# A new order of issue for the pieces of attention and feed-forward, from the third product with w_in on

## The chip, the cores and the metric

One core of one Trainium2 chip runs the kernel. The metric is the device time of one execution in microseconds (us), lower is better. The five engines of the core (TensorE as PE, with its weight loads as PEld; VectorE as DVE; ScalarE as ACT; GpSimd as POOL; SyncE as SP, which here only issues DMAs) each work through an instruction stream of their own, in order, and wait for one another through semaphores.

## The reference

```python
q_s = softmax over d of q;  k_s = softmax over s of k      # 8 batches, 8 heads, 576 rows, 64 wide
kv  = einsum('bhsd,bhse->bhde', k_s, v)
x   = einsum('bhsd,bhde->bhse', q_s, kv)                   # 4608 tokens x 512
h   = x @ w_in                                             # 512 x 2048
g   = maximum(h, 0) + log1p(exp(-abs(h)))                  # softplus
out = g @ w_out                                            # 2048 x 512
```

All arrays are float32.

## The kernel before

**Arithmetic.** The two large products are computed to float32 accuracy on the matrix engine by writing each operand as a high part and a low part (`hi` a rounded copy, `lo` the remainder); one product then is three matmuls, hi·hi, lo·hi and hi·lo, added up in one bank of PSUM. A cast on ACT makes the high part and a subtraction on DVE the low part.

**Tiling.** The 4608 tokens are nine tiles of 512 (t = 0 to 8). The 2048 columns of w_in are sixteen blocks of 128 (j = 0 to 15).

- Tiles 0 to 2 go one by one. `U` (L715) is the product of one tile with one column block, 12 matmuls; `A` (L732) is softplus on ACT; `G` or `H` (L736) splits the result (ACT L740, DVE L743); `O` or `I` (L748) is its product with one block of w_out, 12 matmuls into four banks, `I` a half of it. In the token `U21`, 21 is 16·t + j.
- Tiles 3 to 8 go in three pairs p = 0 to 2, each pair by a scheme of seven products in place of eight (Strassen's). `C p.s.i` (L825) are the pieces of the product with w_in for the s-th of eight double blocks: i = 0 to 6 the products (six matmuls each, L852 to L854, 1.36 us), 7 `spread` (ACT, copies bank 0 to bank 1 between product 0 and products 1 or 2), 8 `take` (ACT, L868, reads bank 1 between products 1 and 3), 9 and 14 softplus out of a bank, 10 `half` (ACT, reads bank 1 between products 3 and 5), 11 and 15 additions on DVE (L875, L879), 12 and 16 softplus in place. `d p.i.s` (L959) are the products with w_out, six matmuls, L966 to L968; `e p.i.s.0` and `.1` (L935) split their right operand (ACT L946, DVE L949); `t` (L929) are differences that the scheme needs; `o` (L970) ends a pair: copies, sums and transposes (L1003) on DVE and ACT, and `store`, each four DMA issues on POOL (L1009).
- `X p.c.name` (L792) prepares the right operands of a pair's `C` products: differences on DVE (L816), casts on ACT (L809), subtractions on DVE (L813).

**Attention.** `k b.h.i` (L462) are the nine steps of one pair of heads (maximum, reduced over the partitions on POOL for later batches, exponent on ACT, product 6 of 20 matmuls at L528), `q` the softmax of the queries, `x t.h.i` (L656) the product of queries and kv (step 3, eight matmuls at L651), its ACT copy (step 6, L675) and, for the first tiles, the split (4, 5).

**Weights.** `T`, `M`, `S`, `J`, `P`, `Q` unpack one column block of both weights from the form in which it was loaded; they run on ACT (about 1.1 us each), DVE (1.2 us) and, with `.1`, POOL (2.5 us). This takes place in the first 150 us.

**Transfers.** `R2.n` (`fetch_sums`, L379) fetches 1 MB of sums of weight blocks for n = 8·p + s into one of two buffers, `x2` and `x0` in turn; so it can start only when the last product with the sums of s − 2 (`C` pieces 1, 3, 4 and 5) has read that buffer, and `C p.s.1` is the first product that needs it. `R0`, `R3`, `R4` fetch other weight parts, `r p.n` (L908) a block of weights for `d` by four DMAs, `n` (`kv_prefetch`, L1056) keys and values ahead of their `k` steps, `L` (`q_load`, L551) the queries of a tile by four DMAs of 256 KB. All of these are issued by SP, in the order of their tokens; the stores of `o` are issued by POOL.

**What sets the order.** The string `ORDER` holds 2304 tokens. The loop at the end of `tile_attn_ffn` hands each to `do` (L1091), which emits its instructions, under `tc.manual_schedule()`: the order of the tokens is the order of issue on every engine. Waits follow from the buffers that the pieces read and write.

Of the kernel before, what the change touches and what calls it, by code (L numbers as in the profile page):

```python
# [9 lines left out]
U8 = mybir.dt.uint8  # L10
U16 = mybir.dt.uint16
U32 = mybir.dt.uint32
# [55 lines left out]
    O16 Y0.1 G18 Y1.0 q2.6 q2.8 k2.0.7 k2.1.7 k2.1.8 U21 A21 Y1.2 k2.2.0 Y0.3 U22 O17 G19 q2.3 D6 Y1.1 k2.0.8 Y1.3 O18
    G20 Y3.0 k2.3.0 O19 A22 G21 O20 G22 k2.3.1 Y3.1 k2.2.1 Y3.2 Y0.4 k2.2.2 q2.5 Y2.0 Y2.1 O21 D8 O22 k2.2.3 k2.3.2
    k2.3.3 k2.3.4 k2.3.5 k2.2.4 q2.7 L3 D15 Y4.0 U23 k2.2.5 Y2.2 Y2.3 k2.3.6 k2.2.6 q2.9 A23 H1.7.0 H1.7.1 k2.2.7  # L70
    k2.3.7 U24 A24 Y2.4 Y2.5 q2.10 U25 Y4.2 O23 U26 H1.8.0 k2.2.8 x2.0.0 Y1.4 H1.8.1 A25 q3.0 q3.1 q3.12 H1.9.0 q2.11
    Y3.3 n k3.0.0 Y2.6 O24 D13 Y2.7 U27 Y3.4 k2.3.8 H1.9.1 x2.2.0 x2.1.0 Y1.5 Y4.1 Y3.5 Y4.3 O25 A26 H1.10.0 Y4.4 n
    Y0.5 k3.1.0 Y3.6 A27 U28 A28 Y1.6 H1.11.0 H1.10.1 x2.1.3 x2.0.4 x2.0.5 O26 Y2.8 Y3.7 H1.12.0 U29 q3.2 Y6.0 q3.3
    H1.11.1 x2.1.4 x2.1.5 x2.3.0 D11 O27 Y0.6 Y0.7 H1.12.1 A29 U30 k3.0.4 k3.0.5 k3.1.4 q3.5 k3.1.5 Y4.5 Y1.7 O28 q3.4
    q3.6 R0.0 H1.13.0 A30 H1.14.0 U31 Y3.8 Y4.6 x2.3.3 A31 q3.7 Y0.8 H1.13.1 L4 O29 H1.14.1 q3.8 x2.2.4 Y6.1 q3.13
    R0.1 x2.2.5 R0.2 x2.3.4 x2.3.5 k3.0.6 y0.0 y0.1 q3.9 H1.15.0 y0.2 y0.3 H1.15.1 k3.1.6 k3.0.7 k3.0.8 U32 A32 n n
    q4.0 q4.1 q4.12 y0.4 R0.3 Y6.2 k3.1.7 O30 H2.0.0 H2.0.1 Y6.3 Y1.8 q4.2 U33 k3.1.8 O31 F1.0 k3.2.0 k3.3.0 R2.0
    k3.2.4 k3.3.4 R0.4 U34 A33 H2.1.0 U35 F1.1 q3.10 k3.3.5 q4.3 k3.2.5 k3.2.6 F1.2 q4.4 F1.3 q4.6 k3.3.6 Y7.0 n Y7.1
    A34 y0.5 y1.0 Y5.0 Y6.4 O32 k3.2.7 k3.2.8 Y6.5 y0.6 k3.3.7 k3.3.8 A35 H2.1.1 y2.0 R0.5 x3.0.0 x3.1.0 O33 R0.6 Y4.7
    Y4.8 U36 Y7.2 H2.2.0 H2.3.0 H2.2.1 O34 y1.1 y1.2 y1.3 y1.4 y0.7 U37 H2.3.1 q3.11 n A36 A37 H2.4.0 x3.2.0 H2.4.1  # L80
    y0.8 x3.1.3 x3.0.6 x3.1.6 x3.3.0 Y5.2 O35 H2.5.0 k4.0.0 k4.1.0 k4.0.4 R0.7 q4.5 U38 O36 x3.3.3 x3.3.6 x3.2.6 U39
    R0.8 q4.7 Y7.3 k4.0.5 y3.0 y3.1 H2.5.1 k4.1.4 k4.1.5 k4.0.6 k4.1.6 y2.1 R0.9 Y7.4 Y7.5 k4.0.7 O37 A38 y3.2 y3.3
    k4.1.7 k4.1.8 y1.5 y3.4 y3.5 H2.6.0 y4.0 y4.1 y4.2 U40 y4.3 H2.6.1 k4.0.8 O38 A39 H2.7.0 U41 n q4.8 y4.4 y1.6
    k4.2.0 Y6.6 Y6.7 n H2.7.1 O39 k4.3.0 y3.6 k4.2.4 y2.2 R0.10 q4.13 Y7.6 R0.11 A40 A41 k4.3.4 Y7.7 k4.3.5 U42 H2.8.0
    Y7.8 R0.12 q4.9 q4.10 k4.2.5 H2.8.1 k4.2.6 k4.2.7 y4.5 H2.9.0 A42 k4.3.6 k4.3.7 O40 k4.2.8 Y6.8 Y5.1 Y5.3 y1.7
    y1.8 y2.3 Y5.4 Y5.5 H2.10.0 y4.6 x4.0.0 U43 H2.9.1 Y5.6 Y5.7 A43 X0.0.hB11 O41 X0.0.lB11 U44 k4.3.8 H2.11.0 R0.13
    H2.10.1 H2.11.1 y4.7 O42 x4.1.0 x4.1.3 x4.0.6 X0.0.T1 y5.0 x4.1.6 A44 q4.11 Y5.8 U45 y5.1 y5.2 x4.2.0 O43 X0.0.hT1
# [5 lines left out]
    C0.0.9 R3.2.0 X0.1.lT1 X0.0.lT4 C0.0.3 C0.0.10 C0.1.0 F2.1 y5.7 X0.1.lT3 C0.1.7 X0.1.T4 X0.1.hT4 X0.0.lT3 C0.0.4
    y5.8 k5.0.0 X0.1.lT4 L5 C0.0.5 R2.2 y7.2 y7.3 C0.1.1 C0.0.11 C0.0.6 k5.1.0 C0.1.8 C0.1.2 k5.0.4 C0.1.3 C0.0.15
    R4.2.0 C0.2.0 F2.2 C0.1.4 R3.3.0 k5.1.4 k5.1.5 C0.1.10 y6.3 y6.4 k5.0.5 k5.0.6 q5.0 q5.1 k5.1.6 C0.1.5 n R2.3
    C0.0.14 C0.2.7 C0.2.1 C0.2.8 C0.1.11 C0.1.6 R4.5.0 k5.0.7 k5.0.8 y6.5 R4.3.0 C0.2.2 R3.4.0 C0.2.3 k5.1.7 k5.1.8
    q5.12 n C0.1.15 R4.4.0 C0.1.9 e0.0.0.0 C0.3.0 q5.2 q5.3 C0.2.10 C0.1.14 C0.2.4 k5.2.0 k5.2.4 C0.3.7 q5.4 C0.2.5
    C0.2.11 q5.5 C0.3.1 R2.4 t0.1.1 C0.2.6 C0.2.15 C0.3.2 R3.5.0 e0.0.1.0 y6.6 y6.7 y6.8 k5.3.0 C0.3.8 C0.3.3 q5.6
    C0.2.9 C0.4.0 C0.3.4 C0.3.10 C0.3.5 C0.2.14 C0.4.7 e0.0.0.1 C0.4.1 k5.3.4 q5.7 C0.3.11 k5.2.5 q5.8 k5.3.5 k5.2.6
    k5.3.6 C0.3.14 C0.3.6 C0.4.8 C0.4.2 C0.4.3 y7.4 y7.5 y7.6 q5.13 C0.3.9 k5.2.7 k5.3.7 k5.3.8 C0.5.0 y7.7 C0.4.4  # L100
    q5.9 q5.10 C0.3.15 L6 q6.0 C0.4.10 C0.5.7 q6.1 k5.2.8 C0.4.11 C0.4.5 x5.0.0 R2.5 C0.5.1 C0.5.8 C0.4.9 C0.4.14
    C0.1.16 C0.4.6 C0.5.2 q5.11 n C0.3.16 C0.5.9 t0.1.2 C0.5.3 k6.0.0 k6.0.4 C0.5.10 R3.6.0 C0.1.12 x5.1.0 C0.6.0
# [5 lines left out]
    e0.0.3.1 C0.7.4 C0.7.11 e0.0.4.0 e0.0.4.1 C0.7.5 d0.0.1 C0.7.6 C0.0.12 q6.6 d0.0.2 X1.0.hB21 e0.0.5.0 k6.2.0
    k6.3.0 t0.1.0 e0.0.5.1 d0.0.3 r0.1 d0.0.4 d0.0.5 q6.5 k6.3.4 e0.0.6.0 e0.0.6.1 d0.0.6 k6.2.4 q6.7 e0.0.7.0 k6.3.5
    e0.0.7.1 X1.0.lB11 k6.2.5 e0.3.0.0 e0.3.1.0 e0.3.0.1 e0.3.1.1 C0.7.14 t0.2.1 k6.2.6 k6.2.7 k6.3.6 e0.3.2.0  # L110
    e0.3.2.1 d0.0.7 C0.6.12 e0.3.3.0 t0.2.0 r0.2 d0.3.0 e0.3.4.0 d0.3.1 e0.3.5.0 C0.7.15 t0.1.7 k6.3.7 C0.7.16 t0.2.2
    o0.spread.0 e0.3.4.1 C0.2.16 e0.3.3.1 d0.3.2 e0.3.6.0 t0.2.3 d0.3.3 o0.spread.1 d0.3.4 r0.5 e0.3.7.0 q6.8 e0.3.5.1
    d0.3.5 e0.1.0.0 e0.1.1.0 e0.3.6.1 t0.2.6 d0.3.6 C0.7.12 e0.3.7.1 d0.3.7 e0.1.0.1 e0.1.1.1 r0.4 d0.1.0 q6.13 t0.2.4
    k6.3.8 r0.6 e0.1.2.0 q6.9 t0.3.1 d0.1.1 r0.7 e0.1.3.0 t0.2.5 e0.1.2.1 q6.10 d0.1.2 e0.1.3.1 d0.1.3 k6.2.8 t0.2.7
    r0.11 n e0.1.4.0 e0.1.4.1 e0.1.5.0 e0.1.5.1 e0.1.6.0 o0.v.0 e0.1.7.0 d0.1.4 e0.2.0.0 x6.0.0 d0.1.5 e0.1.6.1 d0.1.6
    e0.1.7.1 d0.1.7 e0.2.2.0 t0.3.5 e0.2.1.0 e0.2.0.1 X1.1.hB21 o0.u.1 d0.2.0 t0.3.3 e0.2.1.1 d0.2.1 t0.3.2 o0.u.0
# [1100 lines left out]
```

## Time and profile before

| | |
|---|---|
| median of 3 runs | 824.14 us (823.71 to 824.73) |
| the profiled execution | 824.4 us, of which the span of the trace is 822.6 us |
| granted TensorE clock, mean | 0.997 |
| PE busy | 801.7 us, 97% of the span |
| DVE, ACT, POOL busy | 71%, 60%, 14% |
| DMA | 193.74 MB, 236 GB/s over the span |

Times in the rows are microseconds from the start of the span. A row of an engine's timeline is: start, duration, engine, line, operation, output<-input, tile, count, and in brackets the idle time of the engine before it with what ended that. Matmuls overlap: one of 128x512 is shown with some 0.39 us, but the next one starts 0.23 us after it, so time lost on PE is read from start to start.

### The profile page before, as it was taken

The page shows a single profiled execution, that of the slowest core. Times are in us where ns is not written, and L with a number is a line of the kernel's source. Part 1 is how long each engine was busy: PE and PEld are TensorE (multiplying, and loading weights), DVE is VectorE, ACT ScalarE, POOL GpSimd, SP SyncE. Part 2 cuts the span into 40 slices and gives each one's busy share as a digit, 9 for nine tenths or more (in the row PEclk, how much of TensorE's full clock was granted, in tenths as well). Part 3 has the DMA queues.
Part 4 walks back from the last instruction along what each step waited for, and adds up shares of the span by engine and source line. Part 5 has one row for each costly group of instructions (what it writes and reads, how often), then busy time and mean ns, then how long its engine had stood idle before and what let it go on. Part 6 is the DMA issues. An engine that isn't in the chain of part 4 may idle for free.

```text
span 822.6 us, 12090 instructions
## 1 busy us (share of the span) xinstructions
PE 801.7 (97%) x4312; PEld 637.2 (77%) x4312; DVE 584.1 (71%) x934; ACT 497.3 (60%) x824; POOL 116.0 (14%) x211
## 2 busy tenths in 40 slices
...
GB/s 305 374 291 233 262 114 246 212 211 205 270 297 365 230 375 285 310 311 311 178 248 268 129 235 170 299 254 128 244 172 200 165 192 165 281 118 291 264 124 90
DMA packets 118236, 193.74 MB, mean 236 GB/s; under 512 B 8416, under 2 KB 90592, under 8 KB 108960
## 3 DMA queue, kind: packets, MB, share of 16 engines
...
## 4 chain that ended last, share of the span: by engine, by line
PE 82%; DMA 6%; DVE 5%; ACT 3%; POOL 2%; issue 2%; SPq 1%; POOLq 0%; ACTq 0%; DVEq 0%
PE po L852 6%; PE po L968 6%; PE po L853 5%; PE po L854 5%; PE po L966 5%; PE po L967 5%; PE ph L725 4%; PE ph L726 4%; PE po L767 4%; PE ph L727 4%; PE po L769 4%; PE po L768 4%; PE ph L852 3%; PE ph L854 3%; PE ph L853 3%; PE ph L966 3%
## 5 line engine op out<-in xcount | busy, mean ns | idle before, releaser
L1011 POOL DMA_DIRECT2D out<-w x92 | 59.4, 653 | 296.4 <-DVE w L1003 291.9
L767 PE MATMUL po<-w,g_hi 128*128 128x512 f32 x164 | 65.2, 398 | 2.1 <-ACT g_hi L740 2.1
L725 PE MATMUL ph<-x,w 128*128 128x512 f32 x164 | 65.5, 400 | 0.0
L769 PE MATMUL po<-w,g_lo 128*128 128x512 f32 x164 | 64.4, 393 | 0.4 <-DVE g_lo L743 0.3
L949 DVE TENSOR_TENSOR g_lo<-w,g_hi 128x512 fp32r<-128x512 f32 x74 | 49.5, 685 | 20.6 <-ACT g_hi L946 20.6
L768 PE MATMUL po<-w,g_hi 128*128 128x512 f32 x164 | 64.0, 390 | 0.0
L726 PE MATMUL ph<-x,w 128*128 128x512 f32 x164 | 64.0, 390 | 0.0
L727 PE MATMUL ph<-x,w 128*128 128x512 f32 x164 | 63.9, 390 | 0.0
L946 ACT CAST g_hi<-w 128x512 fp32r<-128x512 f32 x74 | 45.5, 619 | 19.1 <-PE po L967 12.8
L933 DVE TENSOR_TENSOR w<-w,w 128x512 f32<-128x512 f32 x72 | 48.5, 683 | 2.7 <-ACT w L886 1.7
L946 ACT CAST w<-w 128x512 fp32r<-128x512 f32 x52 | 31.8, 619 | 24.8 <-PE po L967 18.1
L875 DVE TENSOR_TENSOR w<-po,w 128x512 f32<-128x512 f32 x24 | 16.5, 687 | 40.8 <-PE po L854 40.8
L743 DVE TENSOR_TENSOR g_lo<-g,g_hi 128x512 fp32r<-128x512 f32 x46 | 31.1, 683 | 19.3 <-ACT g_hi L740 19.1
...
L852 PE MATMUL po<-w,x 128*128 128x512 f32 x112 | 44.3, 396 | 0.0
L854 PE MATMUL po<-w,x 128*128 128x512 f32 x112 | 43.8, 391 | 0.0
L853 PE MATMUL po<-w,x 128*128 128x512 f32 x112 | 43.7, 390 | 0.0
L734 ACT ACTIVATE g<-ph 128x512 f32<-128x512 f32 x48 | 28.4, 598 | 24.9 <-PE ph L727 24.6
L477 DVE TENSOR_REDUCE mx<-kvt 128x128 f32<-128x640 f32 x28 | 36.8, 1319 | 4.9 <-DMA kvt<-in_kv_tail 4.0
L949 DVE TENSOR_TENSOR w<-w,w 128x512 fp32r<-128x512 f32 x52 | 35.2, 686 | 6.4 <-ACT w L946 6.2
L767 PEld LDWEIGHTS po<-w,g_hi 128*128 128x128 f32 x164 | 30.8, 188 | 11.4 <-ACT g_hi L740 3.9
L740 ACT CAST g_hi<-g 128x512 fp32r<-128x512 f32 x46 | 28.2, 620 | 18.3 <-PE po L768 13.5
...
## 6 DMA issues: line engine op xcount, KB each, us to landing
x<-sums SPq DMA_DIRECT2D x24, 1024.0 KB, 5.7
...
kept<-w SPq DMA_DIRECT2D x15, 1024.0 KB, 6.9
w<-kept SPq DMA_DIRECT2D x13, 1024.0 KB, 8.7
x<-sums_out SPq DMA_DIRECT2D x44, 256.0 KB, 5.1
w<-kept SPq DMA_DIRECT2D x36, 256.0 KB, 4.6
x<-kept SPq DMA_DIRECT2D x36, 256.0 KB, 4.6
w<-sums_out SPq DMA_DIRECT2D x36, 256.0 KB, 5.7
```

What stands on the lines that cost most here:

```text
L725: nc.tensor.matmul(ph, lhsT=w_hi, rhs=x_hi, start=h == 0, stop=False)
L726: nc.tensor.matmul(ph, lhsT=w_lo, rhs=x_hi, start=False, stop=False)
L727: nc.tensor.matmul(ph, lhsT=w_hi, rhs=x_lo, start=False, stop=h == HP - 1)
L767: nc.tensor.matmul(po, lhsT=g_hi[:, ms], rhs=w_hi, start=j == 0, stop=False)
L768: nc.tensor.matmul(po, lhsT=g_hi[:, ms], rhs=w_lo, start=False, stop=False)
L769: nc.tensor.matmul(po, lhsT=g_lo[:, ms], rhs=w_hi, start=False, stop=j == NJ - 1)
L852: nc.tensor.matmul(ph, lhsT=w_hi, rhs=x_hi, start=c == 0 and i in (0, 4), stop=False, **more)
L853: nc.tensor.matmul(ph, lhsT=w_lo, rhs=x_hi, start=False, stop=False, **more)
L854: nc.tensor.matmul(ph, lhsT=w_hi, rhs=x_lo, start=False, stop=c == 1, **more)
L946: nc.scalar.copy(ring[p, i, s][0], right_of(p, i, s))
L949: engine.tensor_tensor(out=lo, in0=right_of(p, i, s), in1=hi.bitcast(F32), op=ALU.subtract)
L966: nc.tensor.matmul(bank, lhsT=w_hi, rhs=hi, start=begin, stop=False, **more)
```

## The change

Only the string `ORDER` changes. It holds the same 2304 tokens as before, so each engine gets the same instructions; the first 129 tokens (up to `U2`, the third product with w_in) stand as they were, and nearly all behind them stand in another order. The new one comes from a search over a model of the engines in which a wait is for a whole buffer. The matmuls of one piece stay together; what changes is which piece follows which, on every engine and on the SP queue. Of the 2304 tokens the places that matter below, before and after:

```diff
@@ -56,143 +56,142 @@
-    P3 Q3 A1 M5 k1.0.8 U2 S5.1 A2 k1.1.3 k1.1.4 U3 P4 O1 A3 G2 G3 M7.1 O2 T8 J5 Q4 q1.0 P5 Q5.1 q1.1 O3 k1.1.5 M6.1
-    q1.2 T6 J6 U4 q1.4 M8.1 k1.1.6 k1.1.7 T7 J7 U5 P6 A4 Q6 U6 k1.2.0 M10 G4 J8 O4 k1.2.1 P7 Q7 A5 G5 U7 T9 k1.1.8 A6
-    k1.3.0 P8 Q8 k1.3.1 T10 k1.2.2 T12 O5 q1.3 G6 O6 k1.2.3 A7 S10 k1.3.2 M9 k1.3.3 S9 M12.1 J9 q1.6 U8 J10 G7 O7
...
-    O12 x1.1.3 x1.0.4 x1.0.5 G13 G14 Q15.1 P0 x1.2.0 O13 U15 x1.1.4 x1.1.5 x1.3.0 L2 D4 Q0.1 k2.1.0 x1.3.3 x1.2.4
...
-    y2.7 y2.8 X0.1.hB22 O45 X0.1.hB21 y3.7 y3.8 X0.1.lB21 A46 X0.1.lB22 A47 C0.0.0 X0.1.T3 R2.1 n X0.1.hT3 H2.14.0
-    X0.1.T2 H2.14.1 I2.14.0 X0.0.lB21 I2.14.1 H2.15.0 X0.0.T2 X0.0.hT2 X0.0.lT2 X0.1.hT2 X0.1.lT2 C0.0.7 C0.0.1
...
-    x5.3.0 e0.0.1.1 C0.4.12 R2.7 t0.1.4 R4.7.0 C0.7.7 C0.7.1 C0.0.16 C0.5.15 x5.3.3 x5.2.6 x5.3.6 k6.0.6 C0.6.11
-    C0.6.14 R4.6.0 C0.6.6 e0.0.2.0 C0.7.8 C0.6.9 r0.0 n C0.7.2 k6.0.7 e0.0.2.1 C0.6.15 e0.0.3.0 k6.0.8 k6.1.6 C0.7.3
...
-    X1.0.hB22 X1.0.T3 X1.0.lB22 X1.0.T2 X1.0.hT2 X1.0.lT1 X1.0.lT2 X1.0.hT3 x6.3.6 d0.6.0 d0.6.1 e0.6.4.0 o0.flip.0.1
-    o0.store.0.1 e0.6.3.0 e0.6.3.1 C1.0.0 C1.0.7 o0.c12.0 o0.flip.3.0 e0.6.4.1 e0.6.5.0 X1.0.lB21 e0.6.5.1 d0.6.2
-    X1.1.T3 R3.1.1 e0.6.6.0 X1.1.hB22 X1.0.lT3 d0.6.3 e0.6.7.0 r0.13 d0.6.4 X1.1.lB22 X1.1.T2 X1.1.hT2 e0.6.6.1
-    X1.1.hT1 X1.1.T4 e0.6.7.1 d0.6.5 d0.6.6 X1.1.lT2 d0.6.7 k7.0.0 o0.c21.0 C1.0.1 C1.0.2 X1.0.T4 X1.0.hT4 C1.0.8
...
-    C1.0.6 C1.1.2 k7.0.5 C1.1.3 k7.1.5 k7.0.6 q7.1 q7.12 q7.2 q7.3 k7.1.6 C1.0.14 C1.2.0 C1.1.4 L8 o0.flip.2.1 C1.1.10
-    C1.1.5 q7.4 q8.0 R4.1.1 C1.2.7 R2.10 n C1.2.1 C1.0.12 C1.2.8 C1.1.11 C1.1.6 o0.flip.2.0 C1.2.2 q8.1 R3.3.1 n
-    C1.2.3 C1.1.14 C1.0.15 C1.1.9 C1.3.0 k7.2.0 k7.2.4 q7.5 q7.7 k7.3.0 C1.2.4 C1.2.10 o0.store.2.0 C1.3.7 q7.6 C1.2.5
-    R2.11 o0.flip.3.1 C1.3.1 R4.3.1 C1.2.11 R3.4.1 C1.2.6 C1.3.2 R4.5.1 C1.2.9 C1.1.15 q7.8 C1.3.8 R2.12 q7.13 q7.9
...
-    o1.u.0 d1.4.0 e1.4.3.0 t1.3.5 t1.4.5 d1.4.1 e1.4.4.0 e1.4.5.0 e1.4.2.1 d1.4.2 o1.c11.0 X2.0.lB21 e1.4.3.1 e1.4.4.1
-    e1.4.5.1 d1.4.3 d1.4.4 d1.4.5 x8.3.3 x8.2.6 X2.0.hB22 X2.0.lB22 e1.4.6.0 e1.4.6.1 e1.5.0.0 r1.10 e1.4.7.0 x8.3.6
-    e1.5.0.1 e1.4.7.1 X2.1.T1 d1.4.6 X2.1.hB22 X2.1.T3 e1.5.2.0 X2.1.lB22 e1.5.2.1 e1.5.1.0 e1.5.1.1 d1.4.7 o1.c22.1
...
+    P3 Q3 A1 M5 k1.0.8 U2 T8 k1.1.3 k1.1.4 U3 P4 A2 q1.0 S5.1 T9 Q4 A3 G2 M6.1 O1 J5 G3 U4 k1.1.5 P5 O2 T6 M8.1 Q5.1
+    k1.1.6 M7.1 T7 k1.2.0 k1.2.1 J6 J8 P6 k1.1.7 k1.2.2 q1.1 U5 A4 Q6 A5 J7 O3 U6 G4 G5 P7 M10 Q7 k1.1.8 O4 M9 q1.2
+    T12 k1.3.0 U7 S9 q1.3 P8 A6 Q8 J9 T11 T10 A7 G6 q1.4 k1.3.1 O5 D4 P9 k1.2.3 G7 S10 M14.1 k1.2.4 q1.6 k1.3.2 O6
...
+    x1.0.0 A12 G11 U13 Q14 M15.1 k1.2.8 J15 x1.2.0 k1.3.7 P15 k1.3.8 Q15.1 U14 x1.1.0 A13 G12 D3 x1.1.3 O11 x1.3.0 U15
+    G13 x1.0.4 x1.1.4 O12 x1.1.5 A14 x1.0.5 P0 Q0.1 k2.0.0 D6 G14 x1.3.3 D5 x1.2.4 k2.1.0 O13 x1.2.5 x1.3.4 P1 L2
...
+    H2.14.1 X0.0.T2 C0.0.0 I2.14.1 C0.0.7 X0.1.hT3 X0.1.lB21 y7.1 X0.1.hT1 H2.15.0 R4.2.0 X0.1.lB22 X0.1.T2 k5.1.5
+    y5.7 C0.0.2 X0.0.hT3 R4.0.0 I2.14.0 H2.15.1 I2.15.1 X0.1.T4 y7.0 R4.3.0 X0.1.hT2 I2.15.0 k5.1.6 y6.2 X0.1.lT2
...
+    C0.6.9 n C0.0.16 C0.5.12 C0.7.1 C0.7.2 k6.0.0 x5.3.3 C0.6.14 e0.0.2.0 n C0.7.4 e0.0.2.1 k6.0.4 r0.0 q6.6 e0.0.3.0
+    C0.7.8 x5.2.6 k6.1.0 d0.0.0 k6.0.5 C0.6.11 d0.0.1 q6.8 q6.5 R4.6.0 x5.3.6 k6.1.4 e0.0.4.0 q6.7 k6.1.5 C0.7.3
+    C0.7.10 k6.0.6 k6.1.6 d0.0.2 t0.1.4 k6.0.7 e0.0.3.1 r0.1 C0.7.9 e0.0.5.0 d0.0.3 R4.7.0 e0.0.4.1 k6.1.7 e0.0.5.1 n
...
+    X1.1.T1 e0.5.4.0 x6.2.6 X1.0.T1 e0.5.1.1 t0.4.2 d0.5.1 e0.5.2.1 e0.5.4.1 X1.0.T3 x6.3.6 e0.5.3.1 d0.5.2 X1.0.hB22
...
+    d0.5.7 X1.0.hT1 X1.0.hT4 X1.0.lT1 e0.6.4.0 e0.6.3.0 d0.6.1 e0.6.3.1 e0.6.5.0 d0.6.2 d0.6.3 C1.0.2 e0.6.5.1
+    o0.c12.1 X1.1.lT2 e0.6.7.0 X1.1.T4 R3.1.1 X1.1.hT3 e0.6.4.1 X1.1.lT1 d0.6.4 e0.6.6.0 e0.6.6.1 X1.0.lT2 e0.6.7.1
+    R2.9 C1.0.1 C1.0.9 R3.2.1 d0.6.5 o0.flip.1.0 n o0.flip.1.1 d0.6.6 d0.6.7 C1.0.8 o0.c21.0 k7.0.0 X1.1.lT3 o0.c12.0
...
+    X1.0.lT4 X1.1.hT4 X1.1.lT4 C1.1.0 o0.flip.2.0 k7.1.0 C1.1.7 o0.flip.3.1 k7.0.4 L7 o0.c21.1 C1.0.4 k7.1.4 R4.0.1
+    C1.0.3 C1.1.2 C1.0.10 C1.1.1 C1.0.5 R3.3.1 C1.2.0 C1.1.4 C1.0.14 o0.flip.3.0 C1.0.11 R2.10 o0.store.1.0 C1.1.8
+    q7.0 C1.1.3 e1.0.0.0 q7.1 C1.2.7 q7.12 C1.0.6 q7.2 q7.4 C1.0.15 R4.2.1 C1.2.2 C1.1.9 C1.1.10 C1.1.11 C1.1.5 C1.3.0
+    R4.1.1 q7.3 C1.2.9 R4.4.1 R2.11 C1.1.14 e1.0.1.0 C1.2.1 C1.1.6 k7.0.5 C1.3.7 C1.2.4 C1.3.2 L8 C1.3.1 k7.1.5 C1.2.8
...
+    e1.2.7.1 d1.2.6 e1.4.0.1 o1.v.1 o1.u.1 X2.0.lB11 d1.2.7 x8.3.3 e1.4.2.0 e1.4.2.1 d1.4.0 e1.4.1.1 e1.4.3.0 e1.4.4.0
+    e1.4.3.1 d1.4.1 t1.4.6 X2.1.T1 e1.4.4.1 d1.4.2 x8.3.6 e1.4.5.0 t1.4.4 e1.4.6.0 d1.4.3 e1.4.7.0 e1.4.5.1 r1.9
...
+    R2.18 R3.3.2 C2.1.5 C2.3.0 o1.store.0.0 R4.1.2 C2.2.1 C2.2.8 R2.19 C2.1.14 C2.3.7 C2.1.11 C2.1.6 C2.0.15 C2.2.2
+    o1.flip.2.1 C2.4.7 R2.20 C2.5.0 C2.4.1 C2.2.15 C2.4.8 C2.4.2 C2.4.4 R4.3.2 C2.4.3 C2.3.11 t2.1.3 R2.21 C2.0.12
+    C2.5.2 R2.22 C2.6.0 C2.4.14 C2.6.7 C2.5.9 C2.4.6 C2.4.15 C2.5.5 R3.7.2 C2.6.1 C2.6.2 C2.5.4 C2.6.4 R4.6.2 C2.4.12
...
```

## Rows read from the trace of the kernel before

**Rows 1.** Page of the profile, busy time of each engine over the span.

```profile
PE 801.7 (97%) x4312; PEld 637.2 (77%) x4312; DVE 584.1 (71%) x934; ACT 497.3 (60%) x824; POOL 116.0 (14%) x211
```

**Rows 2.** Windows: length, busy of PE, PEld, DVE, ACT, POOL; clock, DMA share, GB/s.

```profile
40.00:80.00 40.00, 40.00 (x182) 29.83 (x181) 35.71 (x44) 38.94 (x48) 5.54 (x6) 1.00 0.87 281
...
480.30:500.30 20.00, 18.42 (x89) 13.82 (x89) 19.09 (x30) 11.03 (x21) 6.98 (x10) 1.00 0.57 166
...
680.00:720.00 40.00, 40.00 (x176) 32.74 (x176) 9.68 (x15) 15.01 (x28) 15.40 (x24) 1.00 0.71 223
```

**Rows 3.** Timeline of PE around the longest wait.

```profile
515.25 0.39 PE L854 MATMUL po<-w,x 128*128 128x512 f32 x1
518.32 0.76 PE L852 MATMUL ph<-x,x 128*128 128x512 f32 x1 [2.68 <-DMA x<-sums]
...
521.34 0.40 PE L853 MATMUL po<-w,spare 128*128 128x512 f32 x1
```

**Rows 4.** Timeline of PE at seven other waits.

```profile
117.64 0.50 PE L767 MATMUL po<-w,g_hi 128*128 128x512 f32 x1 [1.19 <-ACT g_hi L740]
...
247.66 0.50 PE L769 MATMUL po<-w,g_lo 128*128 128x512 f32 x1 [0.31 <-DVE g_lo L743]
...
321.21 0.50 PE L767 MATMUL po<-w,g_hi 128*128 128x512 f32 x1 [0.90 <-ACT g_hi L740]
...
401.35 0.80 PE L528 MATMUL att<-kvt 128*64 128x65 f32 x20 [0.76 <-ACT w L675]
...
493.85 0.50 PE L968 MATMUL po<-w,spare 128*128 128x512 f32 x1 [1.33 <-DVE w L949]
...
637.67 0.50 PE L966 MATMUL po<-w,spare 128*128 128x512 f32 x1 [1.84 <-ACT w L946]
...
650.23 0.50 PE L968 MATMUL po<-w,w 128*128 128x512 f32 x1 [0.25 <-DVE w L949]
```

**Rows 5.** Timeline of the SP queue ahead of the longest wait.

```profile
504.24 2.65 SPq L561 DMA_DIRECT2D qt<-in_q  x4
...
507.64 0.55 SPq L382 DMA_DIRECT2D x<-sums  x1
```

**Rows 6.** DMA issues near 318, 508, 712, 721 us: KB each, us to landing.

```profile
x<-sums SPq DMA_DIRECT2D x1, 1024.0 KB, 8.7
...
x<-sums SPq DMA_DIRECT2D x1, 1024.0 KB, 10.5
spare<-kept SPq DMA_DIRECT2D x1, 256.0 KB, 8.0
...
x<-sums SPq DMA_DIRECT2D x1, 1024.0 KB, 7.5
...
x<-sums SPq DMA_DIRECT2D x1, 1024.0 KB, 4.9
```

**Rows 7.** Page, DMA issues: the first block of weights for a pair's products with w_out.

```profile
x<-kept SPq DMA_DIRECT2D x36, 256.0 KB, 4.6
```

**Rows 8.** Timelines of PE and ACT where one product lies between products 1 and 3.

```profile
497.39 0.39 PE L854 MATMUL ph<-x,x 128*128 128x512 f32 x1
498.97 0.39 PE L852 MATMUL ph<-w,x 128*128 128x512 f32 x1
...
497.45 0.63 ACT L809 CAST w<-w 128x512 fp32r<-128x512 f32 x1 [1.07 <-DVE w L816]
497.98 0.57 ACT L868 COPY g<-ph 128x512 f32<-128x512 f32 x1
```

**Rows 9.** Timelines of POOL, PE and ACT in the stretch of weight unpacking.

```profile
55.15 2.48 POOL L348 TENSOR_TENSOR w<-w,w 128x1024 fp32r<-128x1024 f32 x1 [6.56 <-ACT w L346]
...
61.36 0.50 PE L725 MATMUL ph<-x,w 128*128 128x512 f32 x1
...
52.93 1.15 ACT L313 ACTIVATE w<-w 128x1024 uint32<-128x1024 uint8 x1
```

**Rows 10.** Timeline of PE, the last product.

```profile
816.21 0.39 PE L968 MATMUL po<-x,spare 128*128 128x512 f32 x1
```

231 lines of the change are left out of this document (113 added, 118 removed).

## The prediction

> **What bounds the kernel now.** I read the shares of busy time first: PE is busy for 801.7 us of a span of 822.6 [rows 1]; every other engine has 29% of the span or more to spare. The change neither adds nor removes a matmul, so what it can win is the time in which PE stands, and what it can lose is new standing. The windows say where another engine comes close: ACT is busy 38.94 of 40 us while the weights are unpacked, DVE 19.09 of 20 us between the first and the second pair, and there PE has 18.42 of 20 [rows 2]. Then I read PE's timeline, start to start: in a full stretch a 128x512 matmul starts every 0.226 us (seven starts from 497.39 to 498.97 [rows 8]). A start that comes later, less the small losses of each change of piece, is time lost. Behind the 129 tokens that stay, these come to about 16.0 us:
>
> - 515.25 to 518.32, before `C1.2.1`: 3.07 less 0.23 is 2.84 us, ended by the landing of `R2.10` [rows 3]. Seven intervals then take 3.02 us (518.32 to 521.34) where 1.59 is usual: 1.4 more. Together 4.25.
> - 637.67, between `x8.3.3` and `d1.4.6`: 1.84, and 0.24 in the first starts behind it: 2.1.
> - 493.85, in `d0.6.3` to `d0.6.6`: 1.33 as the bracket has it, 1.5 from start to start, and 0.57 in two steps before it: 2.06.
> - 321.21, around `C0.0.0` and `I2.14.0`: 0.90, that is 1.06 from start to start, and 1.0 in three steps beside it: 2.07.
> - 117.64, `x1.1.3` to `O13`: 1.19 and 0.3 behind it: 1.5.
> - 401.35, `k6.0.6` behind `x5.3.3`: 0.76, with its start 0.9.
> - some ten of 0.15 to 0.5 each, between those at 247.66 and 650.23: 3.1. [rows 4] holds these six points.
>
> Last I read the end: 6.4 us lie between the last product at 816.21 [rows 10] and the end of the span. The last stores and the last products keep nearly their order; I put this part as equal, within 1 us either way.
>
> **The change part by part: what goes.** `R2.10`. Its issue stood at 507.64, just behind the four query loads of `L8`, which held the SP queue from 504.24 for 2.65 us [rows 5], and the transfer took 10.5 us [rows 6]. In the new order `L8` stands behind `R2.11`, and `R2.10` follows `C1.0.5`, the last reader of its buffer, with seven products (9.5 us) up to `C1.2.1`. The 4.25 go. The DMA is then the next to be late; that risk is priced below.
>
> The clock behind this wait: after 2.84 us without a matmul seven intervals went at 0.43 us, the level of 1.2 GHz, while after the 1.84 us at 637.67 they stayed at 0.23 [rows 3, 4]. [...]
>
> `x8.3.3`: `d1.4.0` now follows it, and its split (`e1.4.0.1`) stands ahead of `x8.3.3`; the ACT copy `x8.2.6` is no longer in between. 2.1 go. `x1.1.3` is followed by `O11` and `U15` instead of `O13`: 1.5 go. `H2.14.1` moves ahead of `C0.0.0`, and `C0.0.1` waits until other products have run: 2.07 go. `k6.0.6` moves behind four products and follows the copy that it needs (`x5.3.6`) by one of them: 0.9 go. The ten small ones stand at places that all change; I count them as gone, since new small ones are priced next. With the DVE stretch, counted anew below, 4.25 + 2.1 + 2.06 + 2.07 + 1.5 + 0.9 + 3.1 = 16.0.
>
> **What comes.** (a) Between `d0.5.0` and `C1.1.0` DVE has 43 operations instead of 42, some 26.9 us of work at their start-to-start times, but beside 19 products (25.9 us) instead of 20 and an `x` piece (28.6 us). Before, DVE was full in the second part of this stretch [rows 2], and 2.06 were lost though PE's own work was 1.5 us longer than DVE's (42 operations, 27.1 us). Now DVE's is 1.0 longer. The new sum could have slack from work done earlier (bound 0); if it has none, the 2.06 grow by 2.5 to 4.6. I take 3.5.
>
> (b) Copies of a bank on ACT. Where a `spread`, `take` or `half` lies between two products on the same bank, the old order leaves one product between them at two places only, the new one at 17. One such place shows the room: the last matmul of the first product starts at 497.39, the copy runs from 497.98 to 498.55 behind a cast, and the next product starts on time at 498.97: 0.42 us were left [rows 8]. One more operation ahead of the copy (0.62) would cost 0.2, two would cost 0.8. For 15 places: 0 to 12; I take one more each, the nearest to the row, 15 x 0.2 = 3.0.
>
> (c) `R2.n`. In the old order seven products or more lie between the release of the buffer and its first use, 9.3 us at least. In the new one there are five for six of the fetches (`R2.11`, `R2.14`, `R2.19`, `R2.20`, `R2.22`, `R2.23`): 6.8 us less 0.2 for the issue, 6.6. Of 23 landings between the first, 8.7 us, and the last, 4.9, nine took more than 6.6, three of them in the second pair (10.5 the longest, beside `L8`) and one in the third (7.5) [rows 6]. So 2 x 3/8 + 4 x 1/8 = 1.25 will be late, by 1.2 us at a landing of 7.8: 1.5. The bounds are 0 and six of 10.5 - 6.6 = 3.9 with 1.4 of slow clock each, 32; the upper one would need the old collision six times.
>
> The 7.5 landed while POOL issued stores (15.40 of 40 us [rows 2]), the 4.9 was issued 9.5 us later. The Trainium skill, "DMA: Bandwidth & Descriptors", section "Issuing engines are not separate DMA queues", says that transfers run on the same 16 DMA engines and interleave whichever engine issued them. The new order has `o1.store` among the fetches of the third pair too; if by that rule all four short fetches there land after 7.5, term (c) is 0.75 x 1.2 + 4 x 0.9 = 4.5 and the sum some 820.
>
> (d) Weight unpacking. At 57.63 POOL ends the low part of block 5, and `U5` starts at 61.36: 3.7 us of lead [rows 9]. In the new order two `T` stand further ahead: some 9.1 us of ACT work from 46.5 on, at about 1.1 us per operation [rows 9], then 2.48 on POOL, so 58.1; PE's own pieces from `U2` on reach `U5` at 58.7. The lead shrinks to 0.6. ACT is full here, so an error of one or two operations shows: 0 to 2, I take 0.5.
>
> (e) `r0.0` takes the buffer that `C0.6.5` reads last. Between this and `d0.0.0` lie three products and an `x` piece, 5.2 us, against 0.65 to issue and a landing of 4.6 [rows 7]; before there were four products and three shorter pieces. At a landing of 8.0, as a block of that size shows beside `R2.10` [rows 6], it is 3.4 late. 0 to 3.4; I take 0.5, near the usual landing.
>
> **Sum.** 824.4 - 16.0 + 3.5 + 3.0 + 1.5 + 0.5 + 0.5 = 817.4 for an execution like the profiled one. The 1.8 us outside the span stay. The median of the runs is 0.3 under the profiled time: **817.1 us**.
>
> **The rivals.** *B, nearly all of the waits were matters of order and none come back.* For it: every place of the sum above has its cause in a token that moves. Against it: (a) is a matter of work, not of order. With (a) at its old 2.06 and 1 us for the rest, 824.1 - 16.0 + 3.1 = 811.2: 810 to 812.5.
>
> *C, the waits only move.* The new order keeps PE fed by shorter distances; if ACT and DVE run late in the dense stretches, half to three quarters of the one-product places meet two operations ahead (15 x 0.6 = 9) and DVE costs its 4.6: 824.1 - 16.0 + 9 + 4.6 + 1.5 + 1.0 = 824.2, with a range of 822.5 to 825.8. For it: DVE at 95% and ACT at 97% in two windows. Against it: over the pairs ACT has 60%.
>
> *D, the slower side: late fetches of sums.* Place: the first product that reads them in pairs 1 and 2. Without its term the change gains 16.0 - 7.5 = 8.5. A landing like the 10.5 against 6.6 costs 3.9 and 1.4 of slow clock, 5.3. One leaves 820.9; from the second on the kernel is not faster (826.2); three give 831.5. For it: nine of 23 landings are over the new lead, and a late fetch delays the release for the next. Against it: the one of 10.5 had eight query loads around it.
>
> *E, that the change does not act as it says* can't be here: the order of the tokens is the order of issue.
>
> **Chances.** The forecast (812.5 to 822) 0.50, B 0.15, C 0.15, D 0.20. A measurement of this kernel can tell 0.2%, 1.65 us, from no change. Faster by more than that: the forecast, B and the lower edge of C, 0.67; within it 0.13, the rest of C; slower 0.20. The range reaches into B and over C into D's second late fetch: 810 to 826; the forecast's own is 812.5 to 822.
>
> **What would show it.** No start gap before `C1.2.1`, and 0.23 behind it; none behind the last two `x` pieces; DVE over 95% busy from `d0.5.0` to `C1.1.0`, with some 3 us of gaps named by L949 or L813; gaps at L852 named by L868 or L864 of 0.2 us each in pairs 1 and 2; at most two named by a DMA into x. Gaps of 2 us or more named by that DMA would make it wrong on the slower side, gaps of half a microsecond all along the pairs on that of no change.

## The result, and the profile after

The new order takes 811.06 us (median of 5 runs, 809.80 to 812.18) where the old one takes 824.14 (823.71 to 825.22): ratio 0.9839, 95% interval 0.9825 to 0.9854, that is 13.1 us less. Run once more on another chip it was 0.9832 (0.9811 to 0.9853). The forecast was 817.1, in a range of 810 to 826; the number that came is 6.0 lower, under the forecast's own 812.5 to 822, and is that of rival B.

The profiled execution took 809.8 us, its span is 808.0. The page of the new order, busy time of each engine ([rows 1] before):

```profile
PE 795.7 (98%) x4312; PEld 637.7 (79%) x4312; DVE 581.9 (72%) x934; ACT 499.7 (62%) x826; POOL 119.6 (15%) x211
```

The matmuls are the same, and the time went where PE stood. ACT alone has two instructions more: 42 loads of its table of functions instead of 40, since `A34` (softplus) now stands between the exponents of `k3.2` and `k3.3`. Lines of kernel.py are one lower than before. PE's timeline (start, duration, engine, line, operation, tiles, and in brackets the idle time before) at the places of [rows 3, 4]: first `C1.2.1` behind `C1.3.0`, then `O11` behind `x1.1.3`, `I2.14.1` behind `C0.0.0`, and `d1.4.0` behind `x8.3.3`:

```profile
509.77 0.39 PE L853 MATMUL po<-w,w 128*128 128x512 f32 x1
510.00 0.39 PE L851 MATMUL ph<-x,x 128*128 128x512 f32 x1
...
111.83 1.10 PE L650 MATMUL att<-q_t,kvs 64*64 64x64 f32 x16
112.86 0.50 PE L766 MATMUL po<-w,g_hi 128*128 128x512 f32 x1
...
319.01 0.39 PE L853 MATMUL ph<-w,spare 128*128 128x512 f32 x1
319.24 0.39 PE L766 MATMUL po<-w,g_hi 128*128 128x512 f32 x1
...
616.66 1.09 PE L650 MATMUL att<-q_t,kvs 64*64 64x512 f32 x8
617.68 0.50 PE L965 MATMUL po<-g_hi,x 128*128 128x512 f32 x1
```

No bracket is left at any of them. Of the waits that the new order brought, four are over 0.4 us; the same view has these three, the largest ones:

```profile
351.18 0.50 PE L851 MATMUL po<-w,x 128*128 128x512 f32 x1 [0.32 <-DMA x<-sums]
...
386.18 0.50 PE L851 MATMUL ph<-w,spare 128*128 128x512 f32 x1 [0.44 <-ACT ph L863]
...
560.20 0.80 PE L527 MATMUL att<-kvt 128*64 128x65 f32 x20 [1.26 <-issue]
```

From start to start they cost 0.48 (`C0.3.1`, which waits for `R2.3`), 0.60 (`C0.6.2`, for the bank copy `C0.6.7`) and 1.45 (`k7.3.6`); `k3.3.6` with 0.47 makes it 3.0. The largest is read on ACT: the exponent of `k7.3` stands behind a table load, that of `k7.2`, copies and a cast:

```profile
555.74 1.28 ACT L517 ACT_TABLE_LOAD   x1 [0.99 <-DVE kvt L511]
557.03 0.75 ACT L517 ACTIVATE kvt<-kvt 128x640 f32<-128x640 f32 x1
557.80 1.00 ACT L613 COPY other<-s 32x64 f32<-32x64 f32 x4
558.83 0.62 ACT L945 CAST w<-w 128x512 fp32r<-128x512 f32 x1
559.35 0.74 ACT L517 ACTIVATE kvt<-kvt 128x640 f32<-128x640 f32 x1
```

A step of 0.43 us in `U4` looks like a fifth wait and is none. Behind `O1`, whose matmuls take unsplit float32 operands and start 0.45 apart, the second start of the next piece comes 0.65 after the first in both orders, in `O2` before and in `U4` after (PE's timeline: before, then after):

```profile
51.91 0.82 PE L767 MATMUL po<-spare,g_hi 128*128 128x512 f32 x1
52.56 0.40 PE L768 MATMUL po<-spare,g_hi 128*128 128x512 f32 x1
...
53.57 0.82 PE L724 MATMUL ph<-x,w 128*128 128x512 f32 x1
54.23 0.40 PE L725 MATMUL ph<-x,w 128*128 128x512 f32 x1
```

The account of the two profiled executions, from 824.4 to 809.8, with this step left out on both sides: 15.6 of waits gone, 3.0 of new ones, 2.6 less in the losses under 0.15 us (14.1 to 11.5), 1.1 less from the last product to the end (6.4 to 5.3), and 1.6 more in the head, whose order is the same (`U2` starts at 44.67 instead of 43.03). That makes 14.7 where 14.6 were measured. Of the 2.6, 1.5 belong to the waits: the start that follows a late one is some 0.11 late too, 22 times before and 8 times after.

### The profile page after: what moved, and what is told of

It is laid out like the page before. It is cut to its first block, busy times and chain, and to the rows that moved or that the text cites. A ratio compares the mean times of both kernels' runs of the same rounds, so it can differ in the third digit from the quotient of the medians.

```text
span 808.0 us, 12020 instructions
## 1 busy us (share of the span) xinstructions
PE 795.7 (98%) x4312; PEld 637.7 (79%) x4312; DVE 581.9 (72%) x934; ACT 499.7 (62%) x826; POOL 119.6 (15%) x211
## 4 chain that ended last, share of the span: by engine, by line
PE 94%; DMA 2%; ACT 1%; issue 1%; DVE 1%; POOL 0%; SPq 0%; DVEq 0%
PE po L965 7%; PE po L967 6%; PE po L966 6%; PE po L851 6%; PE po L853 6%; PE po L852 6%; PE po L766 5%; PE ph L724 5%; PE ph L725 5%; PE ph L726 5%; PE po L768 5%; PE po L767 5%; PE ph L851 3%; PE ph L853 3%; PE ph L852 3%; PE ph L965 3%
## 5 line engine op out<-in xcount | busy, mean ns | idle before, releaser
L945 ACT CAST g_hi<-w 128x512 fp32r<-128x512 f32 x74 | 45.8, 621 | 29.8 <-PE po L966 17.2
L479 POOL PARTITION_ALL_REDUCE mx<-mx x20 | 23.0, 1150 | 189.6 <-DVE mx L476 186.4
```

What stands on the lines that cost most here:

```text
L945: nc.scalar.copy(ring[p, i, s][0], right_of(p, i, s))
```

## The experiments

Ratios are to the kernel before on the same chip. Names of runs count from e1 to e12.

**e1, the fetch alone, in the old order.** Old order:

```diff
-    C1.2.0 C1.1.4 L8 o0.flip.2.1 C1.1.10 C1.1.5 q7.4 q8.0 R4.1.1 C1.2.7 R2.10
+    C1.2.0 C1.1.4 R2.10 L8 o0.flip.2.1 C1.1.10 C1.1.5 q7.4 q8.0 R4.1.1 C1.2.7
```

> The old order with one token moved: R2.10 is issued ahead of L8 instead of eight tokens behind it. Theory 1 (each wait is set by the few tokens in front of it, and taking it away is worth its length): the fetch starts at about 504.6 instead of 507.6 and shares the DMA engines with fewer query loads, so it lands before 515.5; the wait of 2.84 us and the 1.4 us at half clock go: 824.1 - 4.25 = 819.9 (819.0 to 820.8). Theory 2 (the old order is balanced, a wait taken away at one place comes back at the next): the query loads land later, the next fetches behind them are late by 2 us or more: 822 to 824.

823.34 us, ratio 0.9985 (0.9967 to 1.0004): no gain that the times can tell. In the trace the wait at `C1.2.1` is gone, `R2.10` landing 3.8 us early, but 0.4 has come at `C1.1.6` and 1.5 at `C1.5.1`; the stretch from `C1.0.0` to `d1.0.0` is 1.8 us shorter instead of 4.25. ACT and PE show why (timelines of e1):

```profile
543.28 0.59 ACT L872 COPY w<-ph 128x512 f32<-128x512 f32 x1 [3.44 <-DMA out<-w]
...
547.19 0.60 ACT L864 COPY po<-po 128x512 f32<-128x512 f32 x1
...
547.84 0.50 PE L852 MATMUL po<-x,x 128*128 128x512 f32 x1 [1.33 <-ACT po L864]
```

A copy on ACT waits for a buffer that the stores of the first pair still read; the bank copy that `C1.5.1` needs stands behind it. Theory 2 has the number, but not the place: of what came back, 0.4 is at a transfer behind the query loads (`R4.1.1`), and 1.5 is in this chain.

**e2, six places in the old order.** Beside the edit of e1:

```diff
-    x1.1.3 x1.0.4 x1.0.5 G13
+    x1.1.3 G13 x1.0.4 x1.0.5
-    C0.0.0 X0.1.T3 R2.1 n X0.1.hT3 H2.14.0 X0.1.T2 H2.14.1 I2.14.0
+    H2.14.0 H2.14.1 C0.0.0 X0.1.T3 R2.1 n X0.1.hT3 X0.1.T2 I2.14.0
-    k6.0.6 C0.6.11 C0.6.14 R4.6.0 C0.6.6
+    C0.6.11 C0.6.14 R4.6.0 C0.6.6 k6.0.6
-    X1.0.lT3 d0.6.3 e0.6.7.0 r0.13 d0.6.4 X1.1.lB22 X1.1.T2 X1.1.hT2 e0.6.6.1 X1.1.hT1 X1.1.T4 e0.6.7.1
+    e0.6.6.1 X1.0.lT3 d0.6.3 e0.6.7.0 r0.13 d0.6.4 X1.1.lB22 e0.6.7.1 X1.1.T2 X1.1.hT2 X1.1.hT1 X1.1.T4
-    x8.3.3 x8.2.6 X2.0.hB22 X2.0.lB22 e1.4.6.0 e1.4.6.1
+    x8.3.3 e1.4.6.0 e1.4.6.1 x8.2.6 X2.0.hB22 X2.0.lB22
```

> The old order with ten tokens moved, at the six largest waits alone: R2.10 ahead of L8; the split e1.4.6 ahead of x8.2.6; G13 ahead of x1.0.4; H2.14 ahead of C0.0.0; k6.0.6 behind C0.6.6; the low parts e0.6.6.1 and e0.6.7.1 ahead of pieces of X1. Theory 1: the waits of these places go and nothing comes for them: 4.25 + 2.1 + 1.5 + 1.5 + 0.9 + 1.5 = 11.75, 812.4 (811 to 814.5), near the whole gain of the new order with 2294 tokens where they were. Theory 2 (DVE is full there and the queues are, so that only a new order of everything helps): at least half comes back at the next pieces, 817 to 821, with new gaps at C1.0.1 to C1.1.0 and at C0.0.1.

820.77 us, ratio 0.9959 (0.9947 to 0.9972): 3.4 us instead of 11.75. All six waits are gone from the trace, and 7.0 us have come just behind them: at `C0.0.1` 1.37, `C1.0.3` 1.18, `C1.1.6` 1.60, `C1.5.1` 1.92, `d1.4.7` 0.95. The two largest (PE's timeline, `C1.1.6` and `C1.5.1`):

```profile
514.07 0.47 PE L852 MATMUL po<-w,spare 128*128 128x512 f32 x1 [1.44 <-DMA spare<-kept]
...
545.12 0.50 PE L852 MATMUL po<-x,x 128*128 128x512 f32 x1 [1.76 <-ACT po L864]
```

Theory 1 falls; theory 2's range has it.

**e3, the loads back ahead of the fetch, in the new order.**

```diff
-    R2.10 o0.store.1.0 C1.1.8 ... C1.3.2 L8
+    L8 R2.10 o0.store.1.0 C1.1.8 ... C1.3.2
```

> The new order with one token moved back: L8, the four query loads, stands directly ahead of R2.10 again. Theory 1: the queue issues the loads for 2.65 us before the fetch, which lands about 10.5 us after an issue at about 503.4, 3.9 us after C1.2.1 could start, with 1.4 us at half clock behind it: 811.1 + 5.3 = 816.4 (814 to 817.5). Theory 2 (in the new order the seven products between release and use cover it): no change, 810.5 to 812.

814.64 us, ratio 0.988 (0.986 to 0.9901), some 3.7 us over the new order, in theory 1's range. The fetch took 11.6 us and PE's timeline has the old picture again, with thirteen intervals at half clock behind it (511.43 to 517.52 for fourteen intervals, 2.9 us more than usual):

```profile
507.78 0.39 PE L853 MATMUL po<-w,w 128*128 128x512 f32 x1
511.43 0.79 PE L851 MATMUL ph<-x,x 128*128 128x512 f32 x1 [3.26 <-DMA x<-sums]
...
517.15 0.53 PE L852 MATMUL po<-w,x 128*128 128x512 f32 x1
517.52 0.39 PE L853 MATMUL po<-w,x 128*128 128x512 f32 x1
```

So this place is worth about what the prediction said (4.25) in the new order: 3.7 by the ratios, 6.0 from `U2` on in the two traces. In the old order it was not.

**e4, the new order mended.**

```diff
-    C0.2.1 C0.3.7 e0.0.0.0 C0.3.2 C0.0.15 C0.2.8 q5.0 C0.3.1 y7.5 q5.1 C0.2.3
+    C0.2.1 C0.3.7 e0.0.0.0 C0.3.2 C0.0.15 C0.2.8 q5.0 C0.2.3 C0.3.1 y7.5 q5.1
-    C0.4.14 k5.3.8 C0.5.14 C0.7.0 C0.6.7
+    C0.4.14 C0.6.7 k5.3.8 C0.5.14 C0.7.0
-    A34 y1.2 k3.3.5
+    k3.3.5 A34 y1.2
-    k7.2.5 q8.13 C1.5.6 e1.0.2.0 C1.7.2 C1.6.11 q8.9 k7.3.5
+    k7.2.5 k7.3.5 q8.13 C1.5.6 e1.0.2.0 C1.7.2 C1.6.11 q8.9
```

> The new order with four tokens moved, at four of the five waits of 0.4 us or more that its trace still has: k7.3.5 (exponent) directly behind k7.2.5, k3.3.5 ahead of A34 (which also saves two loads of ACT's table), the bank copy C0.6.7 directly behind C0.4.14, and C0.2.3 ahead of C0.3.1, which waited for R2.3. Theory 1: 1.45 + 0.47 + 0.60 + 0.48 = 3.0 go: 808.1 (807 to 809.5), faster than both kernels. Theory 2: they come back at the next pieces, 810 to 811.5.

805.77 us, ratio 0.9775 (0.9754 to 0.9796), faster than both. The four waits are gone, none has come, and from `U2` to the end of the span the trace is 3.1 us shorter than that of the new order (763.4 to 760.2). One of the four, 0.48 at `C0.3.1`, is not in the trace of e5, the same new order once more: there `R2.3` landed in time.

**e5, the new order once more.**

> The new order itself once more, as the measure for the others of this call on the same chip. 811.1 (809.8 to 812.2) where the kernel before takes 824.1; its ratio to before 0.984.

808.83 us, ratio 0.9832 (0.9811 to 0.9853), as before.

**e6, the loads ahead of a fetch with a short lead, in the new order.** `L8` stands directly ahead of `R2.11` (`L8 R2.11 C1.1.14 ...`).

> The new order with one token moved: L8 stands directly ahead of R2.11, one of the six fetches with only five products (6.8 us) between the release of its buffer and its first use. Theory 1 (a fetch with that lead is in time only because nothing large is in the queue beside it; beside four query loads it lands after some 10 us, as in the runs with R2.10): 3.5 us late and 1.4 to 2.7 at half clock: 5 to 6 more than the new order, ratio to before 0.990 to 0.992. Theory 2 (the loads cost the same wherever they stand, 3.6 us as ahead of R2.10): ratio 0.988. Theory 3 (five products are enough in any case): ratio 0.984.

815.89 us, ratio 0.9902 (0.9887 to 0.9916): 5.8 over e5 by the ratios, theory 1. `R2.11` took 10.4 us in place of 5.5 (DMA issues, new order and e6), and PE waited:

```profile
x<-sums SPq DMA_DIRECT2D x1, 1024.0 KB, 5.5
...
x<-sums SPq DMA_DIRECT2D x1, 1024.0 KB, 10.4
...
520.08 0.50 PE L851 MATMUL po<-x,x 128*128 128x512 f32 x1 [3.40 <-DMA x<-sums]
```

From start to start that is 3.56, and 1.6 more at half clock behind it; another 0.8 is at `C1.1.6`, for which `R4.1.1` landed late beside the same loads. The price that the prediction set for a late fetch, 5.3, is right; none of the six fetches was late in the new order.

**e7, e1 with the stores moved too.**

```diff
-    C1.3.0 k7.2.0 ... o0.store.2.0 ... o0.store.2.1 ... o0.store.3.0
+    C1.3.0 o0.store.3.0 o0.store.2.1 o0.store.2.0 k7.2.0
```

> The old order with R2.10 ahead of L8, as in the first run, and three store tokens of the first pair's end (o0.store.3.0, 2.1 and 2.0) ahead of k7.2.0 on POOL. Theory 1 (the 1.5 us at C1.5.1 that came when the fetch wait went are a second chain of the old order: kv transfer, maximum on DVE, reduction on POOL, the stores queued behind it on POOL, the buffer that the ACT copy L872 waits for, and the bank copy L864 behind that): with the stores ahead of the reduction it goes, and the fetch edit is worth its full 4.25: ratio to before 0.995 (0.994 to 0.996) instead of 0.9985. Theory 2 (the wait at C1.5.1 has another cause, or the earlier stores delay the fetches as much): 0.998 to 1.000.

825.58 us, ratio 1.0017 (1.0001 to 1.0032): both ranges missed. The wait at `C1.5.1` is gone as theory 1 has it, and the fetches pay for it as the end of theory 2 has it: `C1.1.6` waits for `R4.1.1`, issued at 509.94 and landed 13 us later, where it took 9.5 in e1 (this profiled execution was a long one, 829.4):

```profile
523.38 0.77 PE L852 MATMUL po<-w,spare 128*128 128x512 f32 x1 [5.11 <-DMA spare<-kept]
```

**e8, six places and five repairs, in the old order.** Beside the edits of e2 and e7:

```diff
-    I2.14.1 H2.15.0 X0.0.T2 X0.0.hT2 X0.0.lT2 X0.1.hT2 X0.1.lT2 C0.0.7 C0.0.1 H2.15.1 ... I2.15.0 ... I2.15.1
+    I2.14.1 H2.15.0 X0.0.T2 X0.0.hT2 H2.15.1 X0.0.lT2 X0.1.hT2 X0.1.lT2 C0.0.7 I2.15.0 I2.15.1 C0.0.1
-    C1.0.2 X1.0.T4 X1.0.hT4 C1.0.8
+    C1.0.2 C1.0.8 X1.0.T4 X1.0.hT4
-    R2.10 L8 ... R4.1.1
+    R2.10 R4.1.1 L8
-    x8.2.6 X2.0.hB22 X2.0.lB22 e1.5.0.0 r1.10 e1.4.7.0 x8.3.6 e1.5.0.1 e1.4.7.1
+    e1.4.7.0 x8.2.6 X2.0.hB22 e1.4.7.1 X2.0.lB22 e1.5.0.0 r1.10 x8.3.6 e1.5.0.1
```

> The old order with the six places of the second run and repairs at the five where its trace shows new waits: I2.15 ahead of C0.0.1 (1.37 us there), the copy C1.0.8 ahead of X1.0.T4 and its cast (1.18), R4.1.1 ahead of L8 (1.60), the three store tokens ahead of k7.2.0 (1.92), and e1.4.7 ahead of x8.2.6 (0.95): in all 23 tokens of 2304 moved. Theory 1 (the new waits are chains that stood just behind the old ones, each again with its own few tokens): of the 7.0 us some 6 go, and the kernel comes to within 3 us of the new order: ratio 0.9885 (0.986 to 0.991). Theory 2 (every repair brings the next wait, as the engines are full): ratio 0.993 or more.

820.9 us, ratio 0.9962 (0.9948 to 0.9975), no better than e2. The five are gone, and others have come: for DVE at `C0.0.4` (0.91), `C1.0.4` (0.79), `C1.1.6` (1.03) and `d1.5.1` (1.25), for transfers at `C0.2.1` (0.63), `C1.3.0` (1.57) and `C1.3.1` (2.60; PE's timeline):

```profile
526.59 0.47 PE L852 MATMUL po<-x,x 128*128 128x512 f32 x1 [2.44 <-DMA x<-sums]
```

**e9, DVE work further forward in the dense stretch of the new order.** `o0.flip.0.0`, `0.1`, `1.0` and `1.1` stand ahead of `e0.6.1.1`. Not all of it is new in the stretch, as the expectation has it: `1.0` and `1.1` stood at 487.64 and 488.27 of the new order, ahead of `C1.1.0` (492.32), and come 8 us forward inside it; `0.0` and `0.1` (521.59 and 532.42) are added, 1.25 us.

> The new order with four transposes of the first pair's end (o0.flip.0.0, 0.1, 1.0, 1.1; 0.63 us of DVE each, 2.5 in all) moved from behind C1.0.1 to ahead of e0.6.1.1, into the stretch from d0.5.0 to C1.1.0. Theory 1 (the sum that the prediction made for this stretch: DVE has 26.9 us of work beside 25.9 of PE, so it is the bound there): all of the 2.5 us is lost on PE, ratio to before 0.9865 against 0.9835 of the new order. Theory 2 (DVE has room there, since the piece x6.3.3, on which the operands of the next pair wait, stands eight products earlier than it did, and the work is spread over 28 us where the old order had it in 20): at most 0.7 us is lost, ratio 0.983 to 0.985, and no gap over 0.5 us between d0.6.1 and C1.1.0.

810.64 us, ratio 0.984 (0.9816 to 0.9864); the time can't tell the theories apart. The timelines of DVE and PE can: 2.5 us of transposes stand ahead of a low part, and PE loses 1.6 for it, once (479.40 to 481.24, less 0.23), and nothing more up to `C1.1.0`:

```profile
478.12 2.48 DVE L1002 STREAM_TRANSPOSE w<-w 128x512 f32<-128x512 f32 x4
480.53 0.65 DVE L948 TENSOR_TENSOR g_lo<-w,g_hi 128x512 fp32r<-128x512 f32 x1
...
479.40 0.39 PE L966 MATMUL po<-g_hi,x 128*128 128x512 f32 x1
481.24 0.50 PE L967 MATMUL po<-g_lo,x 128*128 128x512 f32 x1 [1.45 <-DVE g_lo L948]
```

Both theories are off: at this low part DVE was 0.9 us ahead of PE, neither nothing nor 1.8 and more. How much room the whole stretch has this run does not tell.

**e10, every bank copy twice, in the new order.**

```diff
             nc.scalar.copy(bank(1), bank(0))
+            nc.scalar.copy(bank(1), bank(0))
...
             nc.scalar.copy(state["u"], bank(1))
+            nc.scalar.copy(state["u"], bank(1))
...
             nc.scalar.copy(soft[tb, jb], bank(1))
+            nc.scalar.copy(soft[tb, jb], bank(1))
```

> The new order with each of the 72 bank copies on ACT (spread, take, half) issued twice, the same copy into the same place, so that one operation of 0.5 us more stands between a product and the reuse of its bank; 36 us of ACT work are added. Theory 1 (the prediction's price: one operation ahead of the copy costs 0.2 us at each of the 17 places with one product between, and there is one): 3.4 us more where the second copy makes it one, ratio 0.9875 or more. Theory 2 (at these places ACT is idle when the product ends and 0.55 us are left, as the trace of the new order shows): one more copy fits, at most 1 us is lost at them, ratio 0.983 to 0.985.

819.08 us, ratio 0.9939 (0.9918 to 0.996), 8 to 9 us over the new order. At twelve of the 17 places the product after the copy starts 0.06 to 0.12 late and its second matmul another 0.11: 0.2 each, the price of theory 1. The pair of copies at one of them, and PE (the usual start would be 371.18):

```profile
370.02 0.59 ACT L868 COPY g<-ph 128x512 f32<-128x512 f32 x1 [1.25 <-PE ph L853]
370.64 0.59 ACT L869 COPY g<-ph 128x512 f32<-128x512 f32 x1
...
371.28 0.50 PE L851 MATMUL ph<-w,x 128*128 128x512 f32 x1
```

At one place next to nothing was lost. At three, where something else stood ahead of the copy already, it was 0.56 to 1.56 (`C0.3.5`, `C2.6.5`, `C1.2.5`), and 0.34 at `C0.6.3`, where the piece between is a short `x`; 3.4 together. The rest came at places with two products between and where ACT is full otherwise.

**e11, the mended order with `Q4` ahead of `q1.0`.**

> The mended order (k7.3.5 behind k7.2.5, k3.3.5 ahead of A34, C0.6.7 behind C0.4.14, C0.2.3 ahead of C0.3.1) with one token more: Q4 ahead of q1.0 on DVE, for the 0.43 us that U4 waits. Theory 1 (waits of the new order are single, with room behind them): 0.4 less than the mended order, ratio 0.977 (0.975 to 0.979). Theory 2 (the mended order's gain was in part the chip's): ratio 0.980 or more.

806.08 us, ratio 0.9784 (0.9761 to 0.9806), as e4 on another chip: the mended order's gain is not the chip's. The added token did nothing, and could not: the 0.43 in `U4` is the step behind `O1` that the old order has too.

**e12, e1 without the stores.**

```diff
         def store(n, c):
+            if p == 0:
+                return
```

> The old order with R2.10 ahead of L8, as in the first run, and without the 32 store DMAs of the first pair's end (so the outputs of tiles 3 and 4 are left out; its time is to be read beside the first run). Theory 1 (the fetch edit brought 1.3 instead of 4.25 in the old order because the stores of that pair, queued on POOL behind the reduction for k7.2 and k7.3, hold the buffer for the copy L872, and, when they are moved ahead as in the run with the three tokens, fill the DMA engines when R4.1.1 is due): without them both go, no wait over 0.5 us is left between C1.0.0 and d1.0.0, ratio to before 0.995 (0.994 to 0.996). Theory 2 (the query and key loads alone make R4.1.1 and R2.11 late): a wait of 1 us or more stays at C1.1.6 or C1.3.1, ratio 0.997 or more.

822.55 us, ratio 0.9987 (0.9974 to 1.0001): by the time the expectation missed. In the trace, of the waits named, only this is left between `C1.0.0` and `d1.0.0`:

```profile
518.60 0.47 PE L852 MATMUL po<-w,spare 128*128 128x512 f32 x1 [0.30 <-DMA spare<-kept]
```

The stretch takes 88.0 us, against 91.5 in the old order and 89.6 in e1. The head of this execution was the longest of all (`U2` at 45.8), so the span doesn't show it; why the median over 12 runs shows no more of it than in e1 stays open.

## Why the prediction was right, and where its size was off

The forecast of 817.1 missed by 6.0; the stated range holds 811.06 only because it reaches into rival B, to which 0.15 was given. The causes of what goes were right; what comes was put too high.

**What goes, 16.0.** Right, point by point: none of the seven waits or groups is in the new trace (15.6 by the account above, which leaves out the step behind `O1`). For the largest it is shown by undoing it (e3: 3.4 us of wait and 2.9 at half clock came back). What the prediction did not see is that their length is not their worth wherever they stand: in the old order six waits, each taken away by its own few tokens, gave 3.4 us together (e2), and a second round no more (e8). Behind them stood other chains, which then made PE wait for 0.95 to 1.92 us: the stores on POOL behind a reduction, a bank copy behind casts, a 256 KB transfer behind the queries. The new order re-times these as well. It issues sixteen of the first pair's 32 stores from 496.8 on, ahead of the reduction for `k7.2`, where the old one issues eight before 490 and the other 24 from 528.5 on, behind it (ten of them on POOL's timelines: after, then before):

```profile
496.80 6.80 POOL L1010 DMA_DIRECT2D out<-w  x10
```

```profile
528.45 6.41 POOL L1011 DMA_DIRECT2D out<-w  x10
```

The DMA engines are no emptier for it: in windows of 10 us they are busy to 1.06 and 1.04 from 500 to 520, to 1.08 from 510 to 520 before. That what stands first in the queue is now what is needed first is argued, not tried by itself.

**What comes, 9.0 forecast, 3.0 measured.** This is the step that was mis-sized. To these 6.0 come the 2.6 of small losses, for which the sum had no term, and the 1.1 at the end; the longer head (1.6) and the 0.4 that was no wait go the other way. That is the way from 817.4, the sum for a profiled execution, to 809.8.

| term | forecast | measured (over 0.15) | |
|---|---|---|---|
| (a) DVE, `d0.5.0` to `C1.1.0` | 3.5 | 0.0 | |
| (b) bank copies, 17 places | 3.0 | 0.0 | 0.6 at `C0.6.2`, two products between |
| (c) fetches of sums | 1.5 | 0.5 | `R2.3`, none of the six |
| (d) weight unpacking | 0.5 | 0.0 | `U5` starts 0.3 behind its low part (lead forecast 0.6) |
| (e) `r0.0` | 0.5 | 0.0 | |
| not foreseen | 0 | 1.9 | exponents at `k7.3.6`, `k3.3.6` |

(a) The sum took DVE's work against PE's between two marks, as if all of it could be done only there. Of the 43 operations it counted, 38 ran between the marks, 24.1 us of work beside 26.0 of PE: four had run ahead of `d0.5.0`, and one came behind `C1.1.0`. The windows of the new order (length, busy time of PE, PEld, DVE, ACT, POOL) show DVE busy for 94% and then 87%, with PE never idle:

```profile
466.30:480.00 13.70, 13.70 (x65) 11.34 (x61) 12.89 (x22) 10.62 (x22) 0.00 (x0) 1.00 0.61 205
480.00:494.90 14.90, 14.90 (x68) 12.30 (x67) 12.94 (x21) 6.59 (x13) 1.07 (x1) 1.00 0.51 169
```

In the old order `x6.3.3`, on which the next pair's operands wait, ran at 480.3, behind all of `d0.5`, with DVE at 19.09 of 20 us from there [rows 2]; in the new one it runs at 465.3 and the work is spread. In e9 DVE was 0.9 us ahead at one low part, where the sum had it 1.0 behind over all. That the place of `x6.3.3` is what made it is argued, not tried by itself.

(b) The price of 0.2 for one more operation ahead of a copy is right (e10); the assumption that one more stands there was wrong for the most part. At 14 of the 17 places ACT is idle when the product ends, as here, where the copy starts 0.04 us after it and 0.57 are left:

```profile
367.91 0.59 ACT L867 COPY g<-ph 128x512 f32<-128x512 f32 x1 [1.25 <-PE ph L853]
...
368.85 0.39 PE L853 MATMUL ph<-w,spare 128*128 128x512 f32 x1
369.07 0.39 PE L851 MATMUL ph<-w,x 128*128 128x512 f32 x1
```

(c) The six short fetches landed after 4.7 to 5.5 us, 1.1 to 1.9 ahead of their use, since nothing of 1 MB stands beside them in the queue; e6 put it there and paid 5.8. The margin is thin all the same: in e9 `R2.22` took 7.8 (6.4 in e6), and PE lost 1.4 us, in an execution that differs from the new order only far ahead of it; why it took longer there is open.

`R2.21`, issued at 688.8 among twelve stores that POOL issues from 686.2 to 693.9, took 7.4 us, and it has 8.0 us of lead. Of the four short fetches of this pair `R2.22` has four stores beside it and took 5.1, `R2.20` has four in its last 2 us and took 4.9, and the two without any took 4.7 and 4.9. This agrees with the Trainium skill, "DMA: Bandwidth & Descriptors", section "Issuing engines are not separate DMA queues" (transfers interleave on the same 16 DMA engines whichever engine issued them); the 4.5 us that followed from it for term (c) supposed as much traffic beside all four as beside the 7.5. But four stores stood beside the 7.8 of e9 too, so their number alone does not tell when a fetch lands.

**The end.** Put as equal within 1 us, it got 1.1 shorter: POOL has issued its last store at 804.0, ahead of SP's last two at 804.4; in the old order POOL issued until 818.3, and SP's two went at 817.9.

**Rival B** had the number and half of the reason: the waits were matters of order, and (a) was one too. C and D did not come; e6 bears out D's price for one late fetch, and e10 the 0.2 for one operation more, not C's 0.6, which supposes two at many places.
